# Turning keys with VectorE instead of TensorE, and writing every engine's order by hand, in a decode step of two layers

## The chip, the cores and the metric

The kernel runs on one core of one Trainium2 chip. The metric is the device time of one execution in microseconds (us). The span that a profile prints is about 1.8 us shorter than the device time of the same execution. Each kernel was executed several times. A state ("fast" or "slow") is recorded with each run, and ratios compare only fast runs. The engines are TensorE (PE in the profile, its weight loads PEld), VectorE (DVE), ScalarE (ACT), GpSimd (POOL), and SyncE (SP), whose queue starts the loads here.

## The reference, cut to what matters

Two layers of attention and feed-forward network are applied to four sequences of one token each. Both layers use the same weights and the same caches. There are 32 query heads on 8 key/value heads, 4096 cached keys, and a head size of 128, so keys and values of one layer are 33.6 MB each.

```python
def _A_ref(x, k_cache, v_cache, wq, wo):      # x: 4 x 1 x 512
    q = (x @ wq) ...                          # 4 x 32 heads x 1 x 128
    scores = jnp.einsum("bhqd,bhkd->bhqk", q, k) * (Dh ** -0.5)   # 4096 keys
    p = _softmax(scores, axis=-1)
    o = jnp.einsum("bhqk,bhkd->bhqd", p, v)
    return o... @ wo
x = x + _A_ref(_layernorm(x), A_k_cache, A_v_cache, A_wq, A_wo)
x = x + _B_ref(_layernorm(x), B_w_gate, B_w_up, B_w_down)     # gelu(gate) * up, then down
# the same two lines once more: layer 2 has the same caches and weights
```

## The kernel before

Work goes batch by batch (four of them). In layer 1, a group of two key/value heads is loaded, its keys are turned so that the head dimension lies on the partitions, scored, put through softmax, and multiplied with the values. Then come the output projection, the feed-forward network (FFN), the layer-2 queries, and the layer-2 scores on the same turned keys, which stay in memory. The layer-2 values of a batch are loaded again and are used as filler while the next batch runs.

```python
KV_BUFS = 7       # load buffers, each 512 KB, shared by keys and values
def keys(b, kvh):
    kt = ktp.tile([P, C, P], BF16, name="kt", tag="kt")
    for t in range(NT):
        kn = load_kv(A_k_cache, b, kvh, t, "k_t")
        for g in range(CH // TB):
            tp = ps_tp.tile([P, TB, P], BF16, name="tp", tag="tp")
            for i in range(TB):                                    # L218
                nc.tensor.transpose(tp[:, i, :], kn[:, g * TB + i, :], ident_bf[:, :])
            evac(kt[:, c0:c0 + TB, :], tp[:])     # VectorE (L207) or ScalarE (L205)

def scores(b, g, q_bf):                                            # L227
    for s in range(GH):
        for c in range(C):
            nc.tensor.matmul(sc[:, s, c, :], lhsT=KT[kvh][:, c, :],
                             rhs=q_bf[:, b, kvh * rep:(kvh + 1) * rep], start=True, stop=True)

def softmax(sc, pool):
    # colmax on VectorE, gmax on GpSimd, sh = sc - gmax on VectorE, pe = exp(sh) on ScalarE,
    # ssum on VectorE, den on GpSimd, reciprocal on VectorE
    ...
# main loop, cut
for b in range(B):
    for g in range(NGRP):
        for s in range(GH): keys(b, g * GH + s)
        prob1[g] = softmax(scores(b, g, q1_bf), p1p)
        if g > 0: ... values(b, ..., prob1[g - 1], OT_bf)
    ... values of the last group; out_proj_add; ffn; layer_norm; q_proj
    if prob2_prev is not None: ... values(b - 1, ..., OT2_bf)      # layer 2 of the batch before
    prob2_prev = [softmax(scores(b, g, q2_bf), p2p) for g in range(NGRP)]
```

This kernel leaves the order of each engine's instructions to the scheduler of its framework. The text above is therefore not the order in which it runs.

## Time and profile before

| | before |
|---|---|
| device time, median of 4 runs | 376.76 us (375.34 to 378.47) |
| span of the profiled run | 377.3 us |
| first layer-2 queries ready | 97.3 us |
| from there to those of the second, third and fourth batch | 71.2, 78.7, 80.1 us |
| from the last of them to the end (the tail) | 50.0 us |

The profiled run of the kernel before is none of the four timed ones. With 1.8 us added to its span it took about 379.1 us, 0.6% above their median.

The first fence is from the page of the kernel before. It has the span, each engine's busy time, three rows of 40 equal time slices (busy tenths, and GB/s of loads), the chain of work that ended last, and groups of instructions with total busy time, mean ns of one, and idle time before them.

```profile
span 377.3 us, 15723 instructions
PE 275.4 (73%) x7268; PEld 263.8 (70%) x7268; DVE 137.5 (36%) x476; ACT 67.7 (18%) x90; POOL 25.0 (7%) x70
...
PE   0978872645999897578888885697978866785645
...
GB/s 283 413 370 271 387 353 382 406 377 394 83 164 269 384 347 347 386 122 220 279 407 406 356 361 410 244 179 241 404 365 349 377 373 302 156 218 347 407 109 4
...
PE 53%; DMA 16%; DVE 15%; issue 9%; ACT 3%; POOL 3%; SPq 1%; POOLq 0%; ACTq 0%; DVEq 0%
...
L218 PE MATMUL tp<-ident_bf,k_t 128*128 128x128 bf16 x1024 | 97.2, 271 | 1.2 <-DMA k_t<-in_A_k_cache_dram 0.6
...
L205 ACT COPY kt<-tp 128x1024 bf16<-128x1024 bf16 x52 | 52.6, 1012 | 111.0 <-PE tp L218 93.9
L207 DVE COPY kt<-tp 128x1024 bf16<-128x1024 bf16 x76 | 51.7, 687 | 53.2 <-PE tp L218 51.6
```

TensorE is the busiest engine and carries more than half of the chain, and the key transposes (L218) are its costliest group. Their copies out of PSUM are most of ScalarE's work and over a third of VectorE's. Loads reach 413 GB/s in single slices but fall to between 83 and 179 once per batch.

### The profile page before, as it was taken

How to read it: one execution, taken by the hardware profiler on the slowest of the kernel's cores; microseconds unless marked ns; L12 is line 12 of the kernel's file. 1: busy time of each engine (PE TensorE's matmuls, PEld its weight loads, DVE VectorE, ACT ScalarE, POOL GpSimd, SP SyncE). 2: the span in 40 equal slices, each digit the busy share in tenths (PEclk: the TensorE clock that was granted, in tenths of full speed). 3: DMA queues.
4: the chain of work that ended last, by engine and by line, in shares of the span. 5: the costliest groups of instructions: out<-in, count | busy, mean ns of one | idle time of the engine just before them, and what ended most of it. 6: DMA issues, size and time to landing. Idle time of an engine off the chain costs nothing.

```text
span 377.3 us, 15723 instructions
## 1 busy us (share of the span) xinstructions
PE 275.4 (73%) x7268; PEld 263.8 (70%) x7268; DVE 137.5 (36%) x476; ACT 67.7 (18%) x90; POOL 25.0 (7%) x70
## 2 busy tenths in 40 slices
PE   0978872645999897578888885697978866785645
PEld 0878862535998896577788785697978865775545
DVE  0534440032456442333463433334534332351032
ACT  1314230000143330001242230001423400010000
POOL 0000000000112000001100000011010000020000
PEclk9999685555558667555596685555778855555555
DMA  7998999999258999947899999758999998579920
GB/s 283 413 370 271 387 353 382 406 377 394 83 164 269 384 347 347 386 122 220 279 407 406 356 361 410 244 179 241 404 365 349 377 373 302 156 218 347 407 109 4
DMA packets 35762, 115.59 MB, mean 306 GB/s; under 512 B 3176, under 2 KB 9072, under 8 KB 35696
## 3 DMA queue, kind: packets, MB, share of 16 engines
q1 hardware_dynamic: 35696, 114.58, 83.0%
q8 instruction: 57, 0.93, 1.0%
q14 instruction: 9, 0.07, 0.0%
HBM read 114.56 MB, written 0.00 MB: 304 GB/s over the span
## 4 chain that ended last, share of the span: by engine, by line
PE 53%; DMA 16%; DVE 15%; issue 9%; ACT 3%; POOL 3%; SPq 1%; POOLq 0%; ACTq 0%; DVEq 0%
PE tp L218 19%; PE sc L227 14%; DMA v_t<-in_A_v_cache_dram 9%; PE ot L262 7%; DMA wd_sb<-in_B_w_down_dram 6%; PE qps L148 4%; DVE kt L207 2%; PE yT L159 2%; PE hg L170 2%; DVE colmax L233 2%; DMA k_t<-in_A_k_cache_dram 2%; DVE ssum L245 2%; ACT kt L205 2%; ACT pe L243 1%; PE st L114 1%
## 5 line engine op out<-in xcount | busy, mean ns | idle before, releaser
L218 PE MATMUL tp<-ident_bf,k_t 128*128 128x128 bf16 x1024 | 97.2, 271 | 1.2 <-DMA k_t<-in_A_k_cache_dram 0.6
L218 PEld LDWEIGHTS <-k_t 128*128 128x128 bf16 x1024 | 85.2, 125 | 2.0 <-issue 1.0
L262 PE MATMUL ot<-pe,v_t 128*128 128x4 bf16 x2048 | 69.0, 166 | 17.0 <-DMA v_t<-in_A_v_cache_dram 9.7
L262 PEld LDWEIGHTS <-v_t 128*128 128x128 bf16 x2048 | 63.0, 102 | 19.1 <-DMA v_t<-in_A_v_cache_dram 11.0
L227 PE MATMUL sc<-q_bf,kt 128*128 128x4 bf16 x2048 | 69.3, 166 | 9.1 <-DVE kt L207 3.1
L227 PEld LDWEIGHTS <-kt 128*128 128x128 bf16 x2048 | 64.4, 102 | 12.8 <-DVE kt L207 5.3
L205 ACT COPY kt<-tp 128x1024 bf16<-128x1024 bf16 x52 | 52.6, 1012 | 111.0 <-PE tp L218 93.9
L207 DVE COPY kt<-tp 128x1024 bf16<-128x1024 bf16 x76 | 51.7, 687 | 53.2 <-PE tp L218 51.6
L159 PEld LDWEIGHTS <-wo_sb 128*128 128x128 bf16 x640 | 22.4, 102 | 27.8 <-issue 18.6
L159 PE MATMUL yT<-OT_bf,wo_sb 128*128 128x1 bf16 (+1 forms) x640 | 22.2, 165 | 25.5 <-DVE OT_bf L264 16.4
L243 ACT ACTIVATE pe<-sh 128x256 bf16<-128x256 f32 x32 | 13.3, 417 | 99.0 <-DVE sh L239 72.9
L236 POOL PARTITION_ALL_REDUCE gmax<-colmax x32 | 11.8, 369 | 266.6 <-DVE colmax L233 262.0
L264 DVE TENSOR_TENSOR OT_bf<-ot,rden 128x4 bf16<-128x4 f32 x64 | 9.6, 149 | 53.4 <-PE ot L262 53.4
L148 PE MATMUL qps<-xn_bf,wq_sb 128*128 128x1 bf16 (+1 forms) x640 | 18.4, 165 | 8.2 <-DVE xn_bf L136 6.6
L148 PEld LDWEIGHTS <-wq_sb 128*128 128x128 bf16 x640 | 17.9, 104 | 8.8 <-DVE xn_bf L136 7.1
L233 DVE TENSOR_REDUCE colmax<-sc 128x8 f32<-128x256 f32 x32 | 13.6, 424 | 28.0 <-PE sc L227 25.9
L239 DVE TENSOR_TENSOR sh<-sc,gmax 128x256 f32<-128x256 f32 x32 | 13.5, 423 | 11.0 <-POOL gmax L236 10.8
L170 PE MATMUL hg<-xn_bf,wg_sb 128*128 128x1 bf16 (+1 forms) x280 | 8.2, 165 | 10.8 <-DVE xn_bf L136 5.8
L245 DVE TENSOR_REDUCE ssum<-pe 128x8 f32<-128x256 bf16 x32 | 13.3, 415 | 7.5 <-ACT pe L243 7.5
L248 POOL PARTITION_ALL_REDUCE den<-ssum x32 | 13.2, 413 | 39.7 <-DVE ssum L245 39.4
L170 PEld LDWEIGHTS <-wg_sb 128*128 128x128 bf16 x280 | 7.9, 104 | 11.2 <-DVE xn_bf L136 5.0
L194 PEld LDWEIGHTS <-wd_sb 128*128 128x128 bf16 x280 | 8.1, 104 | 8.8 <-issue 5.2
(95 smaller groups left out, 83.1 us busy)
## 6 DMA issues: line engine op xcount, KB each, us to landing
v_t<-in_A_v_cache_dram SPq DMA_DIRECT2D x128, 512.0 KB, 7.1
k_t<-in_A_k_cache_dram SPq DMA_DIRECT2D x64, 512.0 KB, 6.5
wo_sb<-in_A_wo_dram SPq DMA_DIRECT2D x1, 4096.0 KB, 18.8
wq_sb<-in_A_wq_dram SPq DMA_DIRECT2D x1, 3072.0 KB, 15.5
wg_sb<-in_B_w_gate_dram SPq DMA_DIRECT2D x1, 1792.0 KB, 12.3
wu_sb<-in_B_w_up_dram SPq DMA_DIRECT2D x1, 1792.0 KB, 16.3
wd_sb<-in_B_w_down_dram SPq DMA_DIRECT2D x1, 1792.0 KB, 20.9
wq_sb<-in_A_wq_dram SPq DMA_DIRECT2D x1, 1024.0 KB, 5.1
```

The costliest lines, as they stand in the source:

```text
L148: nc.tensor.matmul(qps[:, i, :], lhsT=wq_sb[:, k, m * Dh:(m + 1) * Dh], rhs=xn_bf[:, bs, k], start=(k == 0), stop=(k == KD - 1))
L159: nc.tensor.matmul(yT[:, :, dk], lhsT=wo_sb[:, i, dk * P:(dk + 1) * P], rhs=o_bf[:, bs, i], start=(i == 0 and dk == 0), stop=(i == Hq - 1 ...
L170: nc.tensor.matmul(hg[:, m, :], lhsT=wg_sb[:, k, m * P:(m + 1) * P], rhs=xn_bf[:, bs, k], start=(k == 0), stop=(k == KD - 1))
L205: nc.scalar.copy(out=out_ap, in_=in_ap)
L207: nc.vector.tensor_copy(out=out_ap, in_=in_ap)
L218: nc.tensor.transpose(tp[:, i, :], kn[:, g * TB + i, :], ident_bf[:, :])
L227: nc.tensor.matmul(sc[:, s, c, :], lhsT=KT[kvh][:, c, :], rhs=q_bf[:, b, kvh * rep:(kvh + 1) * rep], start=True, stop=True)
L233: nc.vector.tensor_reduce(out=colmax[:], in_=sc.rearrange("p s c h -> p s h c"), axis=AX.X, op=ALU.max)
L239: nc.vector.tensor_tensor(out=sh[:], in0=sc[:], in1=gmax[:].unsqueeze(2).broadcast_to([P, GH, C, rep]), op=ALU.subtract)
L243: nc.scalar.activation(out=pe[:], in_=sh[:], func=ACT.Exp, scale=scale)
L245: nc.vector.tensor_reduce(out=ssum[:], in_=pe.rearrange("p s c h -> p s h c"), axis=AX.X, op=ALU.add)
L262: nc.tensor.matmul(ot[:], lhsT=v[:, i, :], rhs=pe[:, s, c, :], start=(c == 0), stop=(c == C - 1))
```

## The change

The intent is to take the 1024 key transposes off TensorE and their copies off ScalarE and VectorE. VectorE now transposes 4-byte words (two bf16 numbers each) straight from the loaded tile, in 128 instructions of 128x512 words. The program is laid out for a transpose in blocks of 32x32, with different keys in each of the four partition groups. The queries are therefore spread and masked into 16 columns (four partition groups times four heads), even and odd halves of the words are picked by weight loads with a step of 4 bytes, and four matmuls accumulate. The number of score matmuls, 2048, stays. After the exponential the probabilities sit in the wrong partition groups. Sixteen small TensorE matmuls against 32 columns of an identity matrix swap them, and ScalarE copies the result out. The sum over partitions moves from GpSimd to a matmul with ones.

The order on every engine is now the order of the text (`manual_schedule`), with the layer-2 values of the previous batch handed out in pieces by `fill`. This is the core of the diff. Layout changes of small tiles, the layer norm, the FFN and the projections are cut.

```diff
+    ctx.enter_context(tc.manual_schedule())
-    def keys(b, kvh):            # 32 PE transposes and 4 evictions per head
+    def turn(b, kvh):
+        kt = ktp.tile([P, G8, NB, QD, QS], FP32, name="kt", tag="kt")
+        for t in range(NT):
+            kn = load_kv(A_k_cache, b, kvh, t, "k_t")
+            ...
+            for bb in range(NB):
+                nc.vector.transpose(                                   # L242
+                    out=kt[:, t * gt:(t + 1) * gt, bb].rearrange("p g c j -> p g (c j)"),
+                    in_=kf[:, :, bb])
+    def scores_head(sc, s, kvh, qb):                                   # L251
+        for g in range(G8):
+            for be in range(NB * 2):
+                nc.tensor.matmul(sc[:, s, g, :], lhsT=kt[:, g, be // 2, :, be % 2],
+                                 rhs=qb[:, be, kvh]..., start=(be == 0), stop=(be == NB * 2 - 1))
-    def softmax(sc, pool):
+    def soft_a(sc):    # colmax (VectorE), gmax (GpSimd), subtract (VectorE), exp -> raw (ScalarE)
+    def soft_b(raw, pool):
+        for cc in range(QD):
+            for a in range(QD):
+                nc.tensor.matmul(x[a * QS:(a + 1) * QS, :, :, cc, :],  # L278
+                                 lhsT=ident_bf[:, cc * QS:(cc + 1) * QS],
+                                 rhs=raw[:, :, :, a, :], ...)
+        nc.scalar.copy(out=pe..., in_=x...)                            # L283
+    def soft_c(pe):
+        nc.tensor.matmul(d..., lhsT=ones_bf[:, :], rhs=pe..., ...)     # L289
+        # den: reduction on VectorE (L292), then reciprocal
 # layer 1
+        for g in range(NG):
+            for s in range(GH):
+                turn(b, g * GH + s)
+                scores_head(sc, s, g * GH + s, qb)
+            raw = soft_a(sc)
+            if g > 0:
+                vals.step(GH * NT)
+            pe = soft_b(raw, p1p)
+            prob[g] = (pe, soft_c(pe))
+            ...
 # layer 2
+        for g in range(NG):
+            for s in range(GH):
+                scores_head(sc, s, g * GH + s, qb2)
+            nxt = soft_a(sc)
+            fill(1)
+            if g > 0:
+                pe = soft_b(raw, p2p)
+                prob2[g - 1] = (pe, soft_c(pe))
+            raw = nxt
```

## The prediction

> What bounds the kernel before. The busy row gives TensorE 73% and VectorE 36% of 377.3 us; 115.6 MB in at the 406 GB/s of the best slices is 285 us. The chain of waits is TensorE 53%, DMA 16%, VectorE 15%. By windows, one batch takes 79 us: about 46 us of layer-1 attention (keys transposed, scored, values), 20 us of output projection and FFN, 10 us of layer-2 scores, 3 us between. In the first part DMA share is 0.99 (377 GB/s), in the other two about 0.75 and 0.7.
>
> What the change does. Removed: 1024 PE transposes, which follow each other at 107 ns (16 in 1.73 us in the chain), 110 us of TensorE; 128 evictions (52.6 us ACT, 51.7 us VectorE); 32 POOL sums. Added on VectorE: 128 transposes of 512 words (four per head and batch). No trace here has one. [...] Added on TensorE: 16 small partition swaps per group of two heads[...], one 256-column sum, query spreading. Score matmuls keep their number, 2048; I expect the stride-2 weight load to stay at the 27 ns spacing that scores show now.
>
> Why that does not pay. The order is now the program's on every engine, and VectorE's order makes the group serial: [...]last scores 0.5, maximum 0.47, POOL 0.5, subtraction 0.47, exponential 0.47, [...]ACT copy 0.45, sum 0.4, reduction 0.47, reciprocal 0.2; only then the next group's transposes. That is 10.2 to 10.7 us a group, 42 us for four plus 3.5 us of last values: no better than the 46 us now, though TensorE is freed. FFN: about 19 us, as now (up to nine value tiles at 0.44 us now sit in TensorE's order). Layer-2 scores get worse: ACT's order puts the exponential of group g+1 ahead of the copy of group g, and TensorE waits for that copy before scoring group g+2. A group becomes scores 1.9, maximum 0.47, POOL 0.5, subtraction 0.47, exponential 0.47, copy 0.45, sum 0.4 = 4.7 us, so 19 to 20 us for four against 10 now. Sum: 84 to 86 us a batch against 79.
>
> The first batch (no filler) ends its layer-2 queries a few us earlier than now (about 91 against 97), the tail is about 2 us shorter. Estimate 91 + 3 x 85 + 46 = 392 us, 4% slower; DMA is not the bound.
>
> What would show each step: [...]scores' spacing still 27 ns; layer-1 groups of about 10.5 us with TensorE waiting on VectorE transposes; layer-2 groups of 4 to 5 us with TensorE waiting on the ACT copy and VectorE mostly idle; TensorE busy share well down, to about 55%; mean DMA rate under 300 GB/s.
>
> What would make it wrong: a transpose at 0.4 us would save about 8 us a batch and make it faster than before; at 1.1 us it would cost 15 us a batch. Weight loads at stride 2 taking twice as long cost about 28 us in all. Swaps at 0.1 us each[...] cost 20 us.

Terms are cut from this text: the time of a VectorE transpose and the times of the swaps, for which no trace before the change had a number. The sums still contain them. A layer-1 group came to 10.2 to 10.7 us, of which the terms left add up to 3.9 us; the rest is eight transposes, the swaps and what was not listed. From it follow the 84 to 86 us a batch and 91 + 3 x 85 + 46 = 392 us. Of the terms left, the trace before has the maximum (0.42 us), GpSimd's step (0.37), the subtraction (0.42), the exponential (0.42), the reduction (0.42) and the reciprocal (0.20), and the prediction has about 0.05 us more for each (0.13 for GpSimd's, nothing for the reciprocal). The copy, the sum and the last scores were estimates; after the change they took 0.37, 0.37 and 0.64 us.

## More of the kernel before

The next fence, an answer for stretches of time, shows one batch (after the stretch comes its length; PEclk is the granted TensorE clock as a share of full speed, DMA share the busy share of the DMA engines).

```profile
core 0: us, PE busy (x) PEld busy (x) DVE busy (x) ACT busy (x) POOL busy (x), PEclk, DMA share, GB/s
168.50:179.20 10.70, 8.86 (x326) 8.69 (x324) 3.91 (x13) 1.25 (x3) 1.85 (x5) 0.50 0.64 193
179.20:221.90 42.70, 37.06 (x839) 35.18 (x837) 19.65 (x46) 14.82 (x17) 3.45 (x9) 0.75 0.96 362
221.90:247.20 25.30, 16.81 (x561) 16.17 (x559) 8.27 (x49) 0.63 (x2) 0.76 (x2) 0.55 0.84 313
```

I cut each batch at two marks that every kernel has, the fourth (last) softmax maximum of layer 2 and the fourth of layer 1. The rows are: from the layer-2 queries to the last layer-2 maximum ("L2" below), from there to the last layer-1 maximum of the next batch ("L1"), and from there to the next layer-2 queries ("rest": last values, output projection, FFN, queries). In L1, TensorE is busy 87% of the time (37.06 of 42.7 us) and the DMA engines 96%. Two resources are close to their limits there at once, and a change that frees one of them may meet the other.

## The result, and the profile after

| | before | after |
|---|---|---|
| device time, median of 4 runs each | 376.76 us | 398.94 us (398.03 to 403.87) |
| ratio of fast runs | | 1.0608, 95% interval 1.0532 to 1.0684: slower |
| span of the profiled run | 377.3 us | 396.4 us |
| first layer-2 queries ready | 97.3 us | 94.1 us |
| the three batches after | 71.2, 78.7, 80.1 us | 81.6, 82.7, 84.0 us |
| the tail | 50.0 us | 53.9 us |

A ratio here is the mean time of one kernel's fast runs over the mean of the other's fast runs of the same rounds, so it is not quite the ratio of the medians. The five terms add up to the difference of the spans, but for rounding: -3.1 + 10.3 + 4.0 + 3.9 + 3.9 = 19.0 us. The medians differ by 22.2 us, because each profiled run is one run of several; a stage time is uncertain by some of these 3 us.

This is the page of the changed kernel, with the lines that answer to those above.

```profile
span 396.4 us, 14928 instructions
PE 227.7 (57%) x6848; PEld 206.1 (52%) x6848; DVE 172.3 (43%) x569; ACT 26.4 (7%) x75; POOL 12.5 (3%) x38
...
PE   0334266358445667667546667776456667767455
...
GB/s 259 425 364 328 397 417 416 400 398 81 2 106 224 394 418 416 354 255 181 176 251 265 413 419 415 347 258 125 256 228 396 418 413 347 245 196 161 380 112 2
...
PE 31%; DVE 29%; DMA 26%; issue 8%; ACT 4%; POOL 2%; SPq 0%; POOLq 0%; ACTq 0%
...
L251 PE MATMUL sc<-qb,kt 128*128 128x16 bf16 x2048 | 77.9, 175 | 37.8 <-DVE kt L242 32.5
...
L242 DVE STREAM_TRANSPOSE kt<-k_t 128x512 f32<-128x512 f32 x128 | 77.8, 674 | 9.4 <-DMA k_t<-in_A_k_cache_dram 9.4
...
L278 PE MATMUL x<-raw,ident_bf 128*32 128x64 bf16 x512 | 13.2, 239 | 10.9 <-ACT raw L270 9.6
```

TensorE lost 48 us of busy time and VectorE gained only 35, so the sum of work fell. Yet the kernel is slower. The chain no longer has one owner: it passes between TensorE, VectorE and DMA in nearly equal parts, as a chain of dependent steps across engines would. The same batch by the same three stretches, L2, L1 and rest:

```profile
175.70:191.40 15.70, 10.87 (x384) 10.41 (x382) 5.38 (x21) 1.68 (x5) 1.10 (x3) 1.00 0.59 198
191.40:232.80 41.40, 22.94 (x592) 18.82 (x590) 26.97 (x61) 3.29 (x9) 1.47 (x4) 1.00 0.84 302
232.80:258.40 25.60, 19.23 (x643) 18.60 (x641) 8.11 (x46) 1.16 (x4) 0.37 (x1) 1.00 0.99 383
```

L2 grew from 10.7 to 15.7 us, L1 lost only 1.3 us, and the rest stayed. TensorE's busy share in L1 fell from 87% to 55%, but almost none of that became time, and the loads fell from 362 to 302 GB/s, so neither of the two resources that were close to full before is full in L1 now.

The clock of 1.00 in these rows is no measurement. The trace of the changed kernel, like those of e1 to e7 and e9 to e12, holds no clock record, and the profile then prints 1.00. In the trace of the kernel before, back-to-back 128x4 matmuls start 27 ns apart where the granted clock is 0.5 and 25 ns apart where it is 1.0. In the changed kernel they start 27 ns apart, so I take it that it ran at half clock. For its many small matmuls that is 2 ns in 27, too little to be the cause of the loss.

More than half of the loss, 10.3 of 19.0 us, lies in the first period, which the fences don't show: L2 went from 9.9 to 13.0 us, L1 from 35.2 to 40.1, and rest from 26.1 to 28.5. L1 of the first period has less to load than that of the second (about 10.7 MB in both kernels, from rate times length, against 15.5 MB before and 12.5 MB after). The kernel before made use of that, while the changed kernel needed nearly the same 40 us as in the second period.

The timeline of one layer-1 group, the first of its batch, shows what holds it (start in us, duration in us, engine, line, and in brackets the idle time before).

```profile
202.51 0.42 DVE L261 TENSOR_REDUCE colmax<-sc 128x8 f32<-128x256 f32 x1 [0.63 <-PE sc L251]
203.10 0.37 POOL L263 PARTITION_ALL_REDUCE gmax<-colmax  x1 [10.72 <-DVE colmax L261]
203.50 0.43 DVE L266 TENSOR_TENSOR sc<-sc,gmax 128x256 f32<-128x256 f32 x1 [0.57 <-POOL gmax L263]
204.03 0.38 ACT L270 ACTIVATE raw<-sc 128x256 bf16<-128x256 f32 x1 [8.86 <-DVE sc L266]
204.46 0.40 PE L278 MATMUL x<-raw,ident_bf 128*32 128x64 bf16 x16 [1.99 <-ACT raw L270]
...
204.91 0.37 ACT L283 CAST pe<-x 128x256 bf16<-128x256 f32 x1 [0.50 <-PE x L278]
205.34 0.37 PE L289 MATMUL d<-pe,ones_bf 128*128 128x256 bf16 x1 [0.47 <-ACT pe L283]
205.75 0.43 DVE L292 TENSOR_REDUCE den<-d 128x8 f32<-128x256 f32 x1 [1.81 <-PE d L289]
...
206.32 4.81 DVE L242 STREAM_TRANSPOSE kt<-k_t 128x512 f32<-128x512 f32 x8
...
211.77 0.42 DVE L261 TENSOR_REDUCE colmax<-sc 128x8 f32<-128x256 f32 x1 [0.64 <-PE sc L251]
```

Apart from the scores, most of which run beside the transposes, nothing here overlaps with the next step. From one maximum to the next takes 9.26 us: 3.81 us from the maximum to the first transpose, 4.81 us of transposes for the next group, and 0.64 us for the last scores. The transposes wait for nothing but their place in VectorE's list, because the reduction L292 stands before them. In the layer-2 stage there are no transposes, and the order hurts elsewhere:

```profile
183.07 0.41 PE L278 MATMUL x<-raw,ident_bf 128*32 128x64 bf16 x16
...
183.75 0.43 DVE L266 TENSOR_TENSOR sc<-sc,gmax 128x256 f32<-128x256 f32 x1 [0.57 <-POOL gmax L263]
...
184.30 0.38 ACT L270 ACTIVATE raw<-sc 128x256 bf16<-128x256 f32 x1 [2.61 <-DVE OT_bf L320]
184.58 0.37 ACT L283 CAST pe<-x 128x256 bf16<-128x256 f32 x1
185.00 0.37 PE L289 MATMUL d<-pe,ones_bf 128*128 128x256 bf16 x1 [1.52 <-ACT pe L283]
...
185.16 1.90 PE L251 MATMUL sc<-qb,kt 128*128 128x16 bf16 x64
...
187.10 0.43 DVE L261 TENSOR_REDUCE colmax<-sc 128x8 f32<-128x256 f32 x1 [1.03 <-PE sc L251]
```

ScalarE's copy L283 belongs to the group before and had its input ready (the swaps L278 ended at 183.48), but it stands behind the exponential L270 of the current group. TensorE waits 1.52 us for that copy before it may score the next group. A group therefore takes 4.3 us (maxima at 182.76, 187.10 and 191.42).

The same cut for all kernels, of the second of the three periods in each profiled run, in us:

| kernel | L2 | L1 | rest | period |
|---|---|---|---|---|
| before | 10.7 | 42.7 | 25.3 | 78.7 |
| after | 15.7 | 41.4 | 25.6 | 82.7 |
| e1_auto | 12.8 | 37.4 | 26.5 | 76.7 |
| e2_copy_first | 14.2 | 40.7 | 26.7 | 81.6 |
| e3_early_keys | 26.3 | 29.2 | 28.5 | 83.9 |
| e4_half_turn | 16.3 | 36.2 | 27.2 | 79.8 |
| e5_both | 23.5 | 30.3 | 28.9 | 82.7 |
| e6_pipelined | 24.1 | 28.4 | 28.7 | 81.2 |
| e7_bufs5 | 16.6 | 45.3 | 29.0 | 90.9 |
| e8_before_by_hand | 28.8 | 40.3 | 29.2 | 98.3 |
| e9_lookahead | 14.2 | 33.5 | 28.3 | 76.0 |
| e10_lookahead_auto | 13.2 | 36.8 | 26.9 | 76.9 |
| e11_lookahead_half_v | 12.8 | 30.7 | 25.6 | 69.0 |
| e12_after_half_v | 15.1 | 40.0 | 24.8 | 79.8 |

### The profile page after: what moved, and what is told of

Read it like the earlier page. It is cut to its first block, busy times and chain, and to the rows that moved or that the text cites. A ratio compares the mean times of both kernels' runs of the same rounds, so it can differ in the third digit from the quotient of the medians.

```text
span 396.4 us, 14928 instructions
## 1 busy us (share of the span) xinstructions
PE 227.7 (57%) x6848; PEld 206.1 (52%) x6848; DVE 172.3 (43%) x569; ACT 26.4 (7%) x75; POOL 12.5 (3%) x38
## 4 chain that ended last, share of the span: by engine, by line
PE 31%; DVE 29%; DMA 26%; issue 8%; ACT 4%; POOL 2%; SPq 0%; POOLq 0%; ACTq 0%
DMA v_t<-in_A_v_cache_dram 16%; DVE kt L242 15%; PE sc L251 9%; PE ot L315 6%; DMA wd_sb<-in_B_w_down_dram 5%; DMA k_t<-in_A_k_cache_dram 4%; PE qps L163 3%; PE d L289 3%; ACT pe L283 2%; PE y L226 2%; DVE sc L266 2%; DVE colmax L261 2%; DVE den L292 2%; PE hg L200 2%; POOL gmax L263 2%
## 5 line engine op out<-in xcount | busy, mean ns | idle before, releaser
L251 PEld LDWEIGHTS <-kt 128*128 128x128 bf16 x2048 | 67.3, 105 | 62.2 <-DVE kt L242 41.4
L251 PE MATMUL sc<-qb,kt 128*128 128x16 bf16 x2048 | 77.9, 175 | 37.8 <-DVE kt L242 32.5
L242 DVE STREAM_TRANSPOSE kt<-k_t 128x512 f32<-128x512 f32 x128 | 77.8, 674 | 9.4 <-DMA k_t<-in_A_k_cache_dram 9.4
L320 DVE TENSOR_TENSOR OT_bf<-ot,rden 128x4 bf16<-128x4 f32 x64 | 10.2, 159 | 53.4 <-PE ot L315 53.4
L292 DVE TENSOR_REDUCE den<-d 128x8 f32<-128x256 f32 x32 | 13.6, 425 | 39.1 <-PE d L289 39.1
L270 ACT ACTIVATE raw<-sc 128x256 bf16<-128x256 f32 x32 | 12.3, 384 | 242.7 <-DVE sc L266 123.9
L186 PEld LDWEIGHTS <-wo_sb 128*128 128x128 bf16 x640 | 19.9, 105 | 15.8 <-DMA wo_sb<-in_A_wo_dram 9.7
L289 PE MATMUL d<-pe,ones_bf 128*128 128x256 bf16 x32 | 11.9, 372 | 27.8 <-ACT pe L283 27.8
L261 DVE TENSOR_REDUCE colmax<-sc 128x8 f32<-128x256 f32 x32 | 13.6, 425 | 28.8 <-PE sc L251 28.8
L266 DVE TENSOR_TENSOR sc<-sc,gmax 128x256 f32<-128x256 f32 x32 | 13.8, 433 | 18.5 <-POOL gmax L263 18.5
L186 PE MATMUL y<-OT_bf,wo_sb 128*128 128x1 bf16 x512 | 16.4, 166 | 8.9 <-DMA wo_sb<-in_A_wo_dram 8.9
L278 PE MATMUL x<-raw,ident_bf 128*32 128x64 bf16 x512 | 13.2, 239 | 10.9 <-ACT raw L270 9.6
L278 PEld LDWEIGHTS <-ident_bf 128*32 128x32 bf16 x512 | 8.4, 118 | 13.6 <-issue 13.1
L283 ACT CAST pe<-x 128x256 bf16<-128x256 f32 x32 | 11.9, 370 | 22.8 <-PE x L278 22.8
L226 PE MATMUL y<-H_bf,wd_sb 128*128 128x1 bf16 (+1 forms) x280 | 8.6, 166 | 5.8 <-issue 4.0
## 6 DMA issues: line engine op xcount, KB each, us to landing
wq_sb<-in_A_wq_dram SPq DMA_DIRECT2D x1, 3072.0 KB, 15.7
```

What stands on the lines that cost most here:

```text
L186: nc.tensor.matmul(y[:, :, dk], lhsT=wo_sb[:, i, dk * P:(dk + 1) * P], rhs=rhs, start=(first and i == h0 and dk == 0), stop=(last and i == ...
L242: nc.vector.transpose(out=kt[:, t * gt:(t + 1) * gt, bb].rearrange("p g c j -> p g (c j)"), in_=kf[:, :, bb])
L251: nc.tensor.matmul(sc[:, s, g, :], lhsT=kt[:, g, be // 2, :, be % 2], rhs=qb[:, be, kvh].rearrange("p a h -> p (a h)"), start=(be == 0), s ...
L261: nc.vector.tensor_reduce(out=colmax[:], in_=v, axis=AX.X, op=ALU.max)
L266: nc.vector.tensor_tensor(out=w, in0=w, in1=gmax[:].unsqueeze(2).broadcast_to([P, GH, G8 * QD, rep]), op=ALU.subtract)
L278: nc.tensor.matmul(x[a * QS:(a + 1) * QS, :, :, cc, :], lhsT=ident_bf[:, cc * QS:(cc + 1) * QS], rhs=raw[:, :, :, a, :], start=True, stop= ...
```

## The experiments

My theory was that the new operations cost no time in themselves, and that the hand-written order makes softmax and transposes one serial chain. There were three rivals: that the new operations are dear whatever their order (A), that the VectorE transposes bound the kernel by their sheer time, and that the loads bound it. Twelve kernels ran. Three of them (e4, e11, e12) are wrong. The comparison with the reference does not see errors of this kind in attention, and "correct" is worth little for any of these kernels. The runs e1 to e4, e5 to e8, e9 with e10, and e11 with e12 shared a chip and the runs of the kernel before.

### e1_auto: the new operations without the hand order

```diff
-    ctx.enter_context(tc.manual_schedule())
```

> The changed kernel with the hand order switched off, so that the scheduler orders each engine; the same operations. Order theory (the time is lost because the program's order lets no key transpose of the next batch into the layer-2 score stage, and puts an exponential ahead of a copy): the scheduler puts transposes between the layer-2 softmax steps and alternates exponential and copy, so the 19 to 21 us between the layer-2 queries and the next batch's first transpose go to about 12, and the time to 350-375 us, at or below the kernel before. Rival A (the new operations themselves cost too much: 78 us of transposes, swaps, sums): 390-405 us, as with the hand order. Rival B (the loads and the seven buffers bound it): 390-400 us.

Measured: 375.17 us, ratio 1.0001 (0.990 to 1.010). The same operations in the scheduler's order take as long as the kernel before, so the operations are not what costs 6%, and rival A falls. The gain was not where I had put it: the first period fell from 81.6 to 67.5 us, the other two by 5 to 6 us each, mostly in L1.

The equal totals are a sum of stages that differ. Where L1 has little to load (first period), e1 needs 30.6 us and the kernel before 35.2. In the layer-2 stage e1 is slower from the second period on (12.8 us against 10.7), and its tail is as long as that of the changed kernel (53.8 us; 50.0 before). So part of what L2 and the tail lost goes with the operations even in the scheduler's order.

### e8_before_by_hand: the old operations in the order of their text

```diff
+    ctx.enter_context(tc.manual_schedule())     # added to the kernel before
```

> The kernel before, its operations untouched, with the scheduler switched off so that each engine follows the program's order. Order theory: it too loses the overlap of layer-2 scores and softmax with the next batch's keys and the filling of the FFN by values: 30-70 us more, 405-450 us. Rival A (the new operations are the cost): within 10 us of the kernel before, 370-387 us.

Measured: 434.17 us, ratio 1.1573 (1.152 to 1.163), as expected. This completes a table of two by two:

| median us | scheduler's order | order of the text |
|---|---|---|
| old operations | 375.68 (same rounds as e8) | 434.17 |
| new operations | 375.17 | 398.94 |

The old text was never meant as an order (it puts all layer-2 values ahead of the layer-2 scores, and L2 is 28.8 us), so the upper right cell is no fair hand order. Still, the left column shows that in the scheduler's order the exchange of the operations doesn't move the total (within 1%), and the lower row that the 6% come with this hand-written order. That the operations cost nothing is not shown: in e1 the DMA engines are 97% busy from 176.2 to 222.5 us (376 GB/s), so the loads may hide a cost or a gain.

### e2_copy_first: ScalarE's copy ahead of the next exponential in layer 2

```diff
+            if g > 0:
+                pe = soft_b(raw, p2p)
             nxt = soft_a(sc)
             fill(1)
             if g > 0:
-                pe = soft_b(raw, p2p)
                 prob2[g - 1] = (pe, soft_c(pe))
```

> Only the layer-2 score loop changes: the swaps and ScalarE's copy of group g-1 are put ahead of the softmax of group g, so ScalarE copies before the next exponential. Order theory: a layer-2 group goes from 4.3 us to 3.1-3.4 us, three groups in each of four batches, so 11-14 us less: 385-389 us. Rival A (operations cost): no change beyond 2 us, 397-401 us. Rival B (loads bound): what is gained there is waited for again in the next stage, under 4 us gained, 395-400 us.

Measured: 390.89 us, ratio 1.0378 (1.029 to 1.047): 8 us faster than after, 2 us short of the range. The layer-2 maxima of the second period are now 2.5, 4.8 and 2.9 us apart, where they were 3.0, 4.3 and 4.3: two of the three intervals changed by half a microsecond in opposite directions, and one lost 1.4 us. Between the profiled runs (396.4 and 385.3 us) the three periods gave 3.3, 1.1 and 3.8 us and the tail 4.1. The wait at the copy was real. In the other three layer-2 stages the last two intervals are 3.2 to 3.5 and 2.9 us, where they were 4.3 to 4.8 and 4.3: between 0.9 and 1.5 us less each. The interval of 4.8 us has a different cause, a stop of TensorE two matmuls before the end of the scores, for which the profile shows no wait ("issue"):

```profile
184.54 0.22 PE L251 MATMUL sc<-qb,kt 128*128 128x16 bf16 x2 [1.78 <-issue]
...
184.80 0.42 DVE L261 TENSOR_REDUCE colmax<-sc 128x8 f32<-128x256 f32 x1 [2.77 <-PE sc L251]
```

Without it this interval would be about 3.0 us. What stopped TensorE there stays open.

### e3_early_keys: the next batch's keys turned during layer 2

```diff
-                turn(b, g * GH + s)
+                if b == 0:
+                    turn(b, g * GH + s)
 ...                                         # in the layer-2 loop, after each group
+            if b + 1 < B:
+                for s in range(GH):
+                    turn(b + 1, g * GH + s)
```

> Only the place of the transposes changes: those of the next batch's keys are put into the layer-2 score loop, one group behind the scores that free their buffers; ScalarE's order is left alone. Order theory: layer-2 groups become VectorE-bound at 6.5-7 us (26-28 us a batch instead of 20), layer 1 loses its 4.8 us of transposes a group and falls from 45 to 22-28 us a batch for three batches, so 12-17 us a batch less: 350-365 us. Rival A: the work on VectorE is the same, so under 5 us gained, 393-400 us. Rival B (loads bound): layer 1 keeps 40-45 us a batch, 393-405 us.

Measured: 402.29 us, ratio 1.0682 (1.059 to 1.078). This is a clear miss. VectorE was mostly idle in layer 2, and I had taken that idleness for room. The chain of waits of this kernel in layer 2 (start, length, what) shows what happened:

```profile
185.19 4.76 DVE kt L242 x8
189.95 0.32 DVE colmax L261
...
190.43 0.38 POOL gmax L263
...
190.83 0.43 DVE sc L266
...
192.48 0.44 DVE den L292
...
193.15 1.07 DVE kt L242 x2
...
194.24 3.63 DVE kt L242 x6
197.87 0.32 DVE colmax L261
```

The eight transposes stand as one block between two softmax steps of VectorE's list, and the maximum of the next group, whose scores are ready, waits behind the block. L2 plus L1 is 55.5 us, where it was 57.1 us after: the transposes were moved, not hidden, and "rest" grew by 2.9 us. The idle time of VectorE lay in pieces of about half a microsecond inside the softmax chain (0.57 us while GpSimd works, for example), and a block of 4.8 us doesn't fit into them.

### e4_half_turn: half of the transposes (wrong)

```diff
-            for bb in range(NB):
+            for bb in range(1):
 ...
-                nc.tensor.matmul(sc[:, s, g, :], lhsT=kt[:, g, be // 2, :, be % 2],
+                nc.tensor.matmul(sc[:, s, g, :], lhsT=kt[:, g, 0, :, be % 2],
```

> Wrong result on purpose: only one of two transposes of each key tile is made (64 instead of 128) and the scores read that half twice; loads, matmuls and order are as in the changed kernel. Rival A and the order theory both say that a transpose on the serial chain of a layer-1 group counts in full: 2.4 us less in each of 16 groups, but loads (8 tiles of 1.26 us a group) catch up with it, so 360-375 us. Rival B (loads bound already): 392-399 us.

Measured: 389.89 us, ratio 1.0365 (1.029 to 1.044). This is a miss: 64 transposes fewer at 0.6 us apart (eight in 4.81 us) would be 38 us, and only 9 us came. The first layer-1 group after the stage's start shrank from 9.3 to 6.9 us, while the next two took 10.5 and 10.0 us, where they had taken 9.8 and 11.2 (maxima 195.87, 202.81, 213.28, 223.27). After the first group the chain of waits in that stretch is loads:

```profile
200.37 5.30 DMA v_t<-in_A_v_cache_dram
...
206.33 9.31 DMA v_t<-in_A_v_cache_dram
...
216.31 8.08 DMA v_t<-in_A_v_cache_dram
```

A layer-1 group needs eight tiles of 512 KB, about 4.2 MB, which is 10.1 us, or 1.26 us a tile, at 415 GB/s (the best slices of the changed kernel have 413 to 425 GB/s). Behind the serial chain stands a second bound of nearly the same size. The rival that the transposes bound the kernel by their sheer time asked for the 38 us, and falls.

### e5_both and e6_pipelined: combinations

e5 joins the edits of e2 and e3. e6 adds two more to it: the last group's keys are turned in the next batch's layer-1 groups, and the last batch's own values are taken inside its score loop.

```diff
+            if b > 0 and g < GH:
+                turn(b, (NG - 1) * GH + g)            # e6, layer-1 loop
 ...
+            if not last and g < NG - 1:
+                for s in range(GH):
+                    turn(b + 1, g * GH + s)           # e6, layer-2 loop
+            elif g > 0:
+                own.step(GH * NT)
```

> The two edits of e2 and e3 together: the copy ahead of the next exponential, and the next batch's transposes behind each layer-2 group. In e3 the layer-2 group took 8.0 us, because the transposes stood in the same serial chain (transposes, maximum, exponential, copy, sum, reduction, transposes), so nothing was gained. If that is so, then with the copy first the reduction of group g-1 no longer waits behind the transposes of g-1, and a layer-2 group is VectorE's own work, about 6.8-7.2 us; the two edits together gain more than the sum of the two alone (-8 and +3): 368-382 us. Rival (the loads and their seven buffers bound it, whatever the order): 385-400 us.

> An order meant to beat both: e5, with the transposes of the last two heads moved on into the next batch's first two layer-1 groups so that no group ends the stage with PE waiting for them, and the last batch's values of layer 2 started inside its own score loop. Order theory: layer-2 stage 22-25 us with loads at 350 GB/s or more, layer 1 22-27 us, FFN 18-20 us, so 66-72 us a batch against 83, and the end after the last layer-2 queries 42-47 us against 54: 335-355 us. Rival (loads and buffers bound): over 375 us.

Measured: e5 390.05 us, ratio 1.0391 (1.034 to 1.045); e6 383.48 us, ratio 1.023 (1.018 to 1.028). Both are misses, and both times lie in the range that I had given to the loads as rival. The transposes are still blocks of four or eight, as in e3; that this is the reason is argued and not shown. More than half of e6's gain over e5 is the tail, which fell to 46.2 us (51.9 in e5, 53.9 after); the edit to the last batch was made for that.

### e7_bufs5: five load buffers in the changed kernel

```diff
-KV_BUFS = 7
+KV_BUFS = 5
```

> The changed kernel with five buffers for keys and values in place of seven. Order theory: what two buffers can prefetch over the stage in which none is released is 2 tiles of 1.26 us a batch, and at most as much again where layer 1 meets its loads: 4 batches of 2.5 to 5 us, 408-420 us. Rival (loads and buffers bound everything): a loss in proportion in all stages, over 430 us.

Measured: 434.05 us, ratio 1.1568 (1.152 to 1.162), beyond what my theory allowed and in the range of the loads as bound. I conclude that the changed kernel leans on its buffers far more than I had thought: L1 rose from 41.4 to 45.3 us and "rest" from 25.6 to 29.0. More than seven buffers could not be tried: the build of the changed kernel with eight stops, because the pool `p1p` asks for 1 KB per partition and 0.97 KB is left.

### e9_lookahead and e10_lookahead_auto: transposes one or two at a time

The transposes of the next group are handed out by a generator and put singly into the holes of the current group's softmax. The edits of e2 and of e6's tail are in it as well.

```diff
-    def turn(b, kvh):
+    def turn_steps(b, kvh):          # the same, with a yield after each transpose
 ...
+        ahead.step(1)                # in soft_a, while GpSimd finds the maximum
 ...
-            raw = soft_a(sc)
+            raw = soft_a(sc, ahead)
+            ahead.step(2)            # while ScalarE does the exponential
             if g > 0:
-                vals.step(GH * NT)
+                vals.step(NT)
+                ahead.step(1)
+                vals.step(NT)
             pe = soft_b(raw, p1p)
+            ahead.step(2)            # while ScalarE copies and TensorE sums
             prob[g] = (pe, soft_c(pe))
+            ahead.step(GH * NT * NB) # what is left
```

> By hand again, but the transposes of a group are spread one or two at a time over the holes of the group before it: one between maximum and subtraction, three around the value scalings, two ahead of the sum's reduction, two behind it; those of the next batch's first group go into the layer-2 score loop in the same way; the copy stands ahead of the next exponential, and the last batch's values start inside its score loop. e5 and e6 showed that a whole block of eight transposes only moves the serial chain from one stage to another. Order theory: layer-1 groups fall from 9.9 us to 8-8.5 us (loads of 8 tiles at 1.26 us less what is prefetched), layer-2 groups from 4.3 to 3.3 us, the last part from 54 to 46 us: 335-358 us. Rival (loads and seven buffers bound it, whatever the order): 370-385 us, as e1 and e6.

> The same program as e9, with the scheduler in place of the hand order. Order theory: the scheduler reorders by its own rule and gets near e9, within 3% of it, and below e1 by the 7 us of the last part: 350-370 us. Rival (loads and buffers): 370-380 us, like e1.

Measured: e9 373.56 us (371.12 to 374.95, 6 runs), ratio 0.9899 (0.9855 to 0.9943); e10, which is e9 without the hand order, 374.24 us (median of its three fast runs; a slow one of 381.96 is left out), ratio 0.9932 (0.988 to 0.998). e9 is 25 us below the changed kernel and has the lowest median of the versions that are not wrong, but its interval overlaps those of e1 and e10, and 1% below the kernel before counts as the same. I had expected 335 to 358 us, while the loads as bound gave 370 to 385, and that rival is right about the size. Groups without a wait for loads did become short (6.6 and 6.8 us between maxima, where they were 11.1 and 9.3). The first layer-2 queries come 5.2 us later than in the changed kernel (99.3 us), which was not looked into. The chain of waits of e9 in layer 1 shows what stops the others:

```profile
198.16 5.76 DMA k_t<-in_A_k_cache_dram
...
203.94 1.30 DVE kt L242 x2
...
206.99 8.24 DMA k_t<-in_A_k_cache_dram
```

### e11_lookahead_half_v and e12_after_half_v: half of each value tile loaded (wrong)

```diff
-        dq.dma_start(out=tl[:], in_=src[:, t * CH:(t + 1) * CH])
+        n = CH // 2 if name == "v_t" else CH
+        dq.dma_start(out=tl[:, :n], in_=src[:, t * CH:t * CH + n])
 ...
-                    nc.tensor.matmul(self.ot[:], lhsT=v[:, i, :], rhs=pe[:, s, c, :],
+                    nc.tensor.matmul(self.ot[:], lhsT=v[:, i % (CH // 2), :], rhs=pe[:, s, c, :],
```

> Wrong result on purpose: e9 with half of every value tile loaded (32 of 115 MB less; the matmuls read the loaded half twice, their number and order unchanged). If e9 is at its loads in layer 1 (groups of 10 us, waiting on key loads), those groups fall to 7-8 us, the end of layer 1 and the last part lose their waits on value loads: 10 us a batch and 6-8 us at the end, 325-345 us. If e9 is still held by the serial chain of its order, it stays over 360 us.

> Wrong result on purpose: the same halving of the value loads in the changed kernel. If its layer-1 groups (9.4 to 9.9 us, transposes followed by softmax) are held by the order, they keep that length and only the waits on value loads that the trace shows go (third group, last values, last part, first batch with its weights): 15-28 us less, 371-384 us, and e11 gains clearly more than it. If loads bind it as they do e9, it falls as much as e11, to 350-362 us.

Measured: e11 344.88 us, ratio 0.9246 (0.917 to 0.933); e12 377.26 us, ratio 1.0099 (1.000 to 1.020). Only two of seven runs of the kernel before were fast, so the ratios are weak, and I rely on the medians against e9 (-29 us) and against after (-22 us), and on the profiles.

The two halvings separate the bounds. In e12, with half of the value bytes gone, the four layer-1 groups still take 40.0 us where the changed kernel takes 41.4. They are held by the serial order and not by loads; only the third interval became shorter (9.8 us, where it was 11.2). Of the 21 us between the profiled runs of after and e12, 12.5 us lie in the three periods, 6.2 in the tail and about 2.5 in the start. In the second period e12 gains 2.9 us over after, and e11 7.0 us over e9. Once the order is loosened, loads weigh more. But they weigh in the changed kernel too: the 22 us of e12 are as much as the change had cost, and they come mostly from outside the serial groups. The same halving in the kernel before or in e1 was not run; it would tell how much of their equal times is the loads.

## Why the prediction was right or wrong

The call (4% slower) was right and the time close: 392 us was predicted and 398.94 us measured. The sum was 91 + 3 x 85 + 46. Measured from the trace, it is 94.1 + 248.3 + 53.9, a span of 396.4. The terms erred by +3.1, -6.7 and +7.9 us, so part of the closeness is luck. So is part of the loss per batch: the prediction had about 6 us in each, against 79 us before, while the measured losses are 10.3, 4.0 and 3.9 us, because the first period before took only 71.2 us.

- **The transposes.** The predicted time of one rested on no trace. Measured 0.674 us mean and 77.8 us busy in all, with two queued ones overlapping by about 0.08 us (eight in 4.81 us). An estimate from the trace before would have been close: a 128x4 operation took 0.155 us there (L112) and a reduction of 256 elements 0.42 us (L233), which gives 1.04 ns an element and so 0.69 us for 512. The measured median of 672 ns less the 155 ns leaves 1.01 ns for each of 512 elements. The work taken off TensorE was less than the predicted 110 us: the transposes before start 107 ns apart where the granted clock was 0.5, but 56 ns where it was 1.0.
- **The scores.** Predicted 27 ns spacing with the stride-2 weight load, measured 64 in 1.85 us to the end of the last (from 177.87 us), with 174 ns for one (median), so (1.85 - 0.17) / 63 = 26.7 ns. The weight load with a step of 4 bytes took 105 ns (mean), as did the unstepped load of the values in the same run. Right.
- **The swaps.** The predicted times, and waits feared beside them, rested on no trace. Measured 16 in 0.40 us, cheaper than predicted. Where the swaps (128x32 weights) follow a value matmul (128x128 weights, 24 times), the first starts 95 to 96 ns after it, while value matmuls start 27 ns apart.
- **The layer-1 group.** Predicted 10.2 to 10.7 us, measured 9.3, 9.8 and 11.2 in the second period. The mechanism (VectorE's order makes the group serial) is what the timeline shows, and e1, e9 and e12 confirm it. The third group contains a wait for loads that the prediction did not have.
- **The layer-2 group.** Predicted 4.7 us with TensorE waiting at ScalarE's copy, measured 4.3 to 4.8 in the last two of the three intervals of a batch (1.7 to 3.0 in the first), with that wait of 1.5 us. e2, which removes it, gains 8 us. The mechanism is right.
- **The tail.** Predicted "about 2 us shorter", measured 3.9 us longer. This is the mis-sized term. From the last layer-2 queries to the last maximum takes 15.8 us after (342.4 to 358.2) and took 9.3 before (327.3 to 336.6). What follows the maximum is indeed 2.5 us shorter (38.2 instead of 40.7). The prediction fits this second part; that the slower layer-2 stage occurs in the tail too, as it does in each batch, is missing from it. The scheduler's order does not win it back: e1's tail is 53.8 us.
- **Busy share and load rate.** Predicted TensorE about 55% and under 300 GB/s, measured 57% and 291 GB/s. Right.
- **"DMA is not the bound".** Half right. In layer 1 of the changed kernel the order comes first (e12), but the loads come only a few us behind: the chain that ended last is 26% DMA, two buffers fewer cost 35 us (e7), and shortening the serial chain runs into the loads (e4, e9). The prediction's "a transpose at 0.4 us would save about 8 us a batch" fails for that reason: e4, which halved the number of transposes, saved 2.4 to 3.7 us a batch.

What stays open: in e9 the DMA engines are busy 98% of layer 1 (376 GB/s from 185.1 to 228.4 us) and 71% of the layer-2 scores before it (230 GB/s). Moving bytes from one to the other would, I think, need more buffers, and there is no room for them in this layout. Whether fewer tiles of turned keys would free enough was not tried. Open, too, is why L2 and the tail stay longer with the new operations in the scheduler's order (e1).

## What to carry to other kernels

Before moving work off the busiest engine, ask which chain sets the pace afterwards, and write down the order that each engine will keep. In these runs the transposes were hidden only where single ones fitted the holes of the dependent chain (e9), while a block of eight (4.8 us) between two steps of that chain was paid for wherever it stood (after, e3). Test the operations and the order separately, two by two, and measure the next bound by taking half of its work away on purpose (e11, e12) before promising what a better order will bring.
